# Held-back batch loads, v ahead of q and k, and a longer attention lead in a windowed-attention and feed-forward kernel

## The chip, the cores and the metric

The kernel runs on one core of a Trainium2 chip. TensorE (PE) does the matmuls, VectorE (DVE) and ScalarE (ACT) the elementwise work, and GpSimd (POOL) and SyncE (SP) issue nearly all DMA transfers of this kernel. The time of a run is the device time of that core in microseconds (us). Most comparisons below are between series of up to six runs of one kernel, taken on the same chip in turn with runs of the kernel before; each of the four series of experiments ran on another chip. A run is called slow when it is over 1.5% above the fastest of its kernel; all comparisons use the other runs, called fast. Each run also comes with its mean granted clock of TensorE, where 1.0 is full speed.

## The reference, cut to what matters

```python
# q, k, v: 8 batches x 8 heads x 576 positions x 64
scores = scale * np.matmul(q, k.transpose(0, 1, 3, 2))
scores = np.where(abs(i - j) <= 32, scores, -1e9)         # window of 32 to each side
out    = softmax(scores) @ v
x = out.transpose(0, 2, 1, 3).reshape(4608, 512)          # tokens x model width
h = x @ w_in                                              # 512 -> 2048
g = np.where(h > 0, h, np.exp(np.minimum(h, 0)) - 1)      # ELU
return g @ w_out                                          # 2048 -> 512
```

## The kernel before

A small planner written in Python lists every operation with an engine, a rank and its dependencies, simulates a rough timetable, and emits the instructions of each engine in that order. On the chip each engine keeps its order, and only data dependencies and buffers hold it back. The gates and estimated durations of the plan are not enforced.

The work is cut into 36 pairs of attention blocks (128 tokens each) and 10 token tiles for the feed-forward part (two tiles of 2 pairs, eight of 4). "Lead" is how far, in units of the plan of about a microsecond, a pair's attention is ranked ahead of its tile's feed-forward groups.

```python
PER = 8.0
LEAD = 20.0
def prank(i):                      # rank of the attention of pair i
    return PER * tiles[where[i][0]][0] + PER * (i - tiles[where[i][0]][0]) - LEAD - 16
LQ0, LQD = 52.0, 2.4               # loads of q and k: start and spacing in the plan
HR = sorted((..., ("H", t, fo)) for t ... for fo ...)      # feed-forward matmul groups by rank
def gate(r):                       # the last group ranked before r
    return [n for x, n in HR if x <= r][-1:]
# ... for batches 3 to 7: a gate in the plan alone, nothing on the chip
x = need - LQ0 + LQD * (2 * j + (nm == "q"))
deps += gate(x)
P.op(("LQ", b, nm, j), "POOL", 0.9, x, deps, lambda ...: load_nat(b, nm, j), ...)
# ...
def load_nat(b, nm, j):            # GpSimd issues the load of 128 rows of q or k
    ...
    nc.gpsimd.dma_start(out=live["N", nm, b][0:n, j, :]..., in_=src[128 * j:128 * j + n])
def XQ(b, nm, j):                  # SyncE turns them into qT, kT with a DMA transpose
    nc.sync.dma_start_transpose(dst, live["N", nm, b][0:n, j, :])
def load_v(b, qb):                 # GpSimd loads v; SyncE then makes shifted copies (vw<-vw)
    nc.gpsimd.dma_start(out=vt[r:r + hi - lo, qb, :, 0:D], in_=vb[lo:hi])
def X(i):                          # attention result of pair i, transposed to xt
    ...
    if i >= NPX:                   # NPX = 8
        nc.sync.dma_start_transpose(dst, xs)
        return
    pt = psT_p.tile(...)           # pairs 0 to 7: on TensorE, through the one psT bank
    ...
```

So SyncE's queue carries, in one order, the transposes of q and k (`kT<-bf`, `qT<-bf`), those of the attention result (`xt<-xs`), the shifted v copies and the outputs. The first feed-forward matmul of a tile needs the `xt` transpose of all its pairs. The buffers that TensorE writes are named ps: psS for scores, psO for attention times v, psT for transposes (one bank), psH for the first feed-forward matmul (three banks), psY for the second.

The softmax here doesn't subtract the row's maximum and nothing guards it: scores larger than these inputs give would overflow.

## Time and profile before

| | kernel before |
|---|---|
| median of the first runs | 338.19 us (336.65 to 339.34) |
| span of the profiled run, clock | 334.4 us, 1.000 |
| TensorE (PE) busy | 305.8 us |
| PE waits for `xt` | 7.1 us, four times |
| PE waits for `y` (output copies) | 2.3 us, six times |
| PE waits for the first q and k | 8.1 us |
| loads of k (128 KB), issue to landing | 8.4 us |

The prediction shows the main lines of this profile. One further view helps: the timeline of GpSimd (POOL) while it issues batch 5's loads. Columns: start us, length us, engine, line, operation, tile, and in brackets the idle time before it with what ended it.

```profile
98.72 0.88 POOL L304 DMA_DIRECT2D bf<-in_k_dram  x1 [8.84 <-DMA kT<-bf]
99.59 0.78 POOL L322 DMA_DIRECT2D vw<-in_v_dram  x1
100.40 0.97 POOL L304 DMA_DIRECT2D bf<-in_q_dram  x1
101.36 0.88 POOL L304 DMA_DIRECT2D bf<-in_k_dram  x1
...
```

GpSimd waits 8.84 us for a buffer (`kT<-bf` must have read it) and then issues load after load, one every 0.9 us. This is a burst.

### The profile page before, as it was taken

Reading aid. Unit: us, or ns where it says so; the run is one execution under the profiler, and the core shown is the slowest. Engines: PE = TensorE matmul, PEld = TensorE weight load, DVE = VectorE, ACT = ScalarE, POOL = GpSimd, SP = SyncE. Lnnn points to the kernel's source line nnn. Section 1 sums busy time; section 2 is a strip of 40 time slices with the busy share of each in tenths; the row PEclk is TensorE's granted clock in tenths of the full one; section 3 lists DMA queues with packets and bytes.
Section 4 is the critical chain, followed back from the end, with each engine's and each line's share of the span. In section 5 each row is a group of like instructions: output and inputs, shape, how many; then the busy total and the mean of one; then the engine's idle time right before and its main releaser. Section 6 shows DMA issues by size and latency. Waiting matters only on the chain.

```text
span 334.4 us, 7358 instructions
## 1 busy us (share of the span) xinstructions
PE 305.8 (91%) x2896; PEld 160.8 (48%) x2896; DVE 212.0 (63%) x500; ACT 195.5 (58%) x333; POOL 94.6 (28%) x130
## 2 busy tenths in 40 slices
PE   1589999799989998999799979999999999899995
PEld 1477666545544444444344434444444444344442
DVE  4586696568958776677576656667666766455400
ACT  2258997687755553655266636665666566465611
POOL 8944456964318500850095000000000000000000
PEclk9999999999999999999999999999999999999999
DMA  7999999999999998999999973633362111100021
GB/s 98 148 195 208 193 195 178 165 140 155 146 156 181 169 155 115 155 165 155 129 152 170 148 120 78 144 94 80 79 114 71 40 64 49 47 33 31 31 94 63
DMA packets 140369, 41.02 MB, mean 123 GB/s; under 512 B 125360, under 2 KB 135856, under 8 KB 140336
## 3 DMA queue, kind: packets, MB, share of 16 engines
q0 software_dynamic: 91872, 18.36, 72.9%
q1 hardware_dynamic: 48320, 22.08, 35.5%
q8 instruction: 22, 0.36, 0.5%
q10 hardware_dynamic: 144, 0.13, 0.1%
q14 instruction: 11, 0.09, 0.1%
HBM read 36.70 MB, written 9.44 MB: 138 GB/s over the span
## 4 chain that ended last, share of the span: by engine, by line
PE 71%; DMA 14%; DVE 6%; ACT 5%; issue 1%; SPq 1%; POOL 1%; ACTq 0%; POOLq 0%
PE psH L438 32%; PE psY L481 26%; DMA xt<-xs 10%; PE psO L391 4%; PE psS L358 3%; DMA bf<-in_k_dram 2%; DMA vw<-vw 2%; DVE xs L406 2%; PE psT L272 2%; ACT e L446 1%; PE psS L481 1%; PE psO L481 1%; PE psT L481 1%; ACT f L456 1%; ACT pu L366 1%
## 5 line engine op out<-in xcount | busy, mean ns | idle before, releaser
L438 PE MATMUL psH<-xt,w_in_sb 128*128 128x512 bf16 (+1 forms) x640 | 146.8, 360 | 7.4 <-DMA xt<-xs 7.1
L446 ACT ACTIVATE e<-psH 128x512 f32<-128x512 f32 (+1 forms) x160 | 88.3, 554 | 99.3 <-PE psH L438 94.9
L481 PE MATMUL psY<-w_out_sb,g 128*128 128x512 bf16 x528 | 132.9, 379 | 2.3 <-ACT y L491 2.3
L438 PEld LDWEIGHTS <-w_in_sb 128*128 128x128 bf16 x640 | 60.0, 99 | 65.9 <-issue 7.5
L481 PEld LDWEIGHTS <-g 128*128 128x128 bf16 x576 | 52.9, 98 | 58.8 <-issue 3.1
L464 DVE SCALAR_TENSOR_TENSOR g<-f,psH 128x512 bf16<-128x512 bf16 (+1 forms) x72 | 45.0, 625 | 32.9 <-ACT f L456 32.6
L458 DVE TENSOR_SCALAR f<-e 128x512 bf16<-128x512 f32 (+1 forms) x88 | 37.8, 429 | 39.2 <-ACT e L446 39.2
L467 DVE TENSOR_TENSOR g<-psH,f 128x512 bf16<-128x512 f32 (+1 forms) x88 | 56.5, 642 | 2.8
L456 ACT ACTIVATE f<-e 128x512 bf16<-128x512 f32 (+1 forms) x72 | 42.0, 583 | 2.1
L366 ACT ACTIVATE pu<-psS 128x1024 bf16<-128x1024 f32 x36 | 36.8, 1021 | 7.3 <-PE psS L358 5.9
L322 POOL DMA_DIRECT2D vw<-in_v_dram x40 | 33.8, 854 | 22.3 <-PE psH L438 4.0
L304 POOL DMA_DIRECT2D bf<-in_k_dram x25 | 21.6, 866 | 45.8 <-DMA kT<-bf 41.3
L391 PEld LDWEIGHTS <-pm 128*128 128x128 bf16 x576 | 27.0, 101 | 13.6 <-DMA vw<-vw 0.7
L406 DVE TENSOR_TENSOR xs<-psO,rc 128x256 bf16<-128x256 f32 x68 | 28.9, 424 | 2.4
L391 PE MATMUL psO<-vw,pm 128*128 128x65 bf16 x544 | 28.9, 196 | 0.7 <-DMA vw<-vw 0.4
L379 DVE TENSOR_TENSOR pm<-pu,masks 128x512 bf16<-128x512 bf16 x72 | 27.1, 418 | 3.2 <-ACT pu L366 3.2
L304 POOL DMA_DIRECT2D bf<-in_q_dram x25 | 21.8, 871 | 8.1 <-DMA bf<-in_q_dram 2.5
L404 DVE RECIPROCAL rc<-psO 128x4 f32<-128x4 f32 x68 | 12.3, 181 | 18.4 <-PE psO L391 17.8
L491 ACT COPY y<-psY 128x512 f32<-128x512 f32 x33 | 18.8, 570 | 4.5 <-PE psY L481 4.5
L358 PE MATMUL psS<-qT,kT 64*128 64x64 bf16 (+1 forms) x640 | 17.0, 199 | 3.1 <-ACT pu L366 1.8
L358 PEld LDWEIGHTS <-kT 64*128 64x128 bf16 (+1 forms) x640 | 12.1, 102 | 14.9 <-issue 11.9
L272 PEld LDWEIGHTS <-bf 64*64 64x64 bf16 x432 | 10.2, 123 | 14.4 <-DMA bf<-in_q_dram 5.8
(46 smaller groups left out, 87.6 us busy)
## 6 DMA issues: line engine op xcount, KB each, us to landing
out_dram<-y SPq DMA_DIRECT2D x35, 256.0 KB, 2.4
vw<-vw SPq DMA_DIRECT2D x12, 260.0 KB, 6.5
vw<-in_v_dram POOLq DMA_DIRECT2D x24, 128.0 KB, 11.7
bf<-in_k_dram POOLq DMA_DIRECT2D x20, 128.0 KB, 8.4
bf<-in_q_dram POOLq DMA_DIRECT2D x20, 128.0 KB, 8.8
w_in_sb<-in_moe_w_in_dram POOLq DMA_DIRECT2D x4, 512.0 KB, 10.0
w_out_sb<-in_moe_w_out_dram POOLq DMA_DIRECT2D x4, 512.0 KB, 13.9
bf<-in_q_dram POOLq DMA_DIRECT2D x6, 288.0 KB, 11.3
```

Of the source, the lines that this page charges most:

```text
L304: nc.gpsimd.dma_start(out=live["N", nm, b][0:n, j, :].rearrange("p (h d) -> p h d", d=D), in_=src[128 * j:128 * j + n])
L358: nc.tensor.matmul(psS[p0:p1, h % 2, s, hp, :], lhsT=kT[b % NKB][base:base + 64, hp, c:c + p1 - p0], rhs=rhs, start=True, stop=True)
L366: nc.scalar.activation(pu, live.pop(("S", i)), AX.Exp, scale=SCALE)
L391: nc.tensor.matmul(o[:, j, :], lhsT=p[:, h, s * QB:s * QB + 128], rhs=vw[b % NVB][:, qb, h, :], start=(s == 0), stop=(s == 1))
L406: nc.vector.tensor_mul(live["X", i][:, g * HP:(g + 1) * HP, :], o[:, :, 0:D], rb)
L438: nc.tensor.matmul(ps, lhsT=w_in_sb[:, do, fo * 128:(fo + 1) * 128], rhs=xts[t][:, do, :], start=(do == 0), stop=(do == NDO - 1))
L446: nc.scalar.activation(e, ps, AX.Exp)
L456: nc.scalar.activation(f, e, AX.Relu, bias=1.0, scale=-1.0)
L458: nc.vector.tensor_scalar(f, e, -1.0, 0.0, ALU.add, ALU.min)
L464: nc.vector.scalar_tensor_tensor(gs[t][:, fo, :], f, -1.0, ps, ALU.mult, ALU.max)
L467: nc.vector.tensor_tensor(gs[t][:, fo, :], ps, f, ALU.max)
L481: nc.tensor.matmul(ps, lhsT=gs[t][:, fo, c * 128:(c + 1) * 128], rhs=w_out_sb[:, fo, :], start=(fo == 0), stop=(fo == NFO - 1))
```

## The change

The intent was to make the loads of batches 3 to 7 spread out as the plan has them, so that the DMA transposes meet fewer loads, and to give these transposes more time before TensorE needs them.

```diff
+    scr = const.tile([1, 1], BF16)
...
-    def load_nat(b, nm, j):
+    def hold(g):
+        for _, t, fo in g:
+            nc.gpsimd.tensor_copy(scr, gs[t][0:1, fo, 0:1])
+
+    def load_nat(b, nm, j, g):
+        hold(g)
...
-    def load_v(b, qb):
+    def load_v(b, qb, g):
+        hold(g)
...
-    LEAD = 20.0
+    LEAD = (20.0, 28.0)
+    NLEAD = 8
...
-        return PER * tiles[where[i][0]][0] + PER * (i - tiles[where[i][0]][0]) - LEAD - 16
+        return PER * tiles[where[i][0]][0] + PER * (i - tiles[where[i][0]][0]) - LEAD[i >= NLEAD] - 16
...
-    LQ0, LQD = 52.0, 2.4
-    XQ0, XQD = 36.0, 3.5
+    LQ0, LQD = 64.0, 2.4
+    XQ0, XQD = 38.0, 3.0
...
-    HR = sorted((PER * tiles[t][0] + 2 * fo * tiles[t][1] / 4, ("H", t, fo))
+    HR = sorted((PER * tiles[t][0] + 2 * fo * tiles[t][1] / 4, ("GG", t, fo))
...
-                x = need - LQ0 + LQD * (2 * j + (nm == "q"))
+                n = 2 * j + (nm == "q")
+                x = need - LQ0 + LQD * (n + 5 if b > XB or n >= NV3 else n)
...
-            x = need - LQ0 + LQD * (10 + qb / 2)
+            x = need - LQ0 + LQD * (qb / 2 + (NV3 if b == XB else 0))
```

`hold` copies one element of a finished feed-forward group (`g`, written by VectorE), so GpSimd can't issue the load behind it before that group exists. The cut part has a new order of the first loads (a list called RING), and new estimates of DMA durations and of how transfers share the DMA engines in the planner.

## The prediction

> **What bounds the kernel now.** I read the totals of the page first. TensorE (PE) is busy for 305.8 of 334.4 us, at full granted clock, and no other engine passes 63%.
>
> ```profile
> span 334.4 us, 7358 instructions
> PE 305.8 (91%) x2896; PEld 160.8 (48%) x2896; DVE 212.0 (63%) x500; ACT 195.5 (58%) x333; POOL 94.6 (28%) x130
> ```
>
> So only the 28.6 us in which PE stands idle can be won, as long as its work stays the same. The second view, the waits of PE alone, says what those 28.6 us are. Its columns are the waiting instruction, what released it, total us, times, longest:
>
> ```profile
> PE psH L438 <- DMA xt<-xs: 7.1, 4, 2.3
> PE psT L272 <- DMA bf<-in_q_dram: 5.6, 2, 5.4
> PE psH L272 <- DMA bf<-in_k_dram: 2.5, 2, 2.2
> PE psY L481 <- ACT y L491: 2.3, 6, 1.0
> PE psT L272 <- ACT xt L427: 1.9, 3, 0.7
> PE psS L358 <- ACT pu L366: 1.8, 2, 1.1
> PE psT L421 <- ACT kT L290: 1.5, 2, 0.7
> ...
> PE psO L391 <- DMA vw<-vw: 0.4, 1, 0.4
> ```
>
> The two waits for q and k (8.1 us) belong to the first 12 us, when the first inputs are in flight. The largest wait after that is L438, the first feed-forward matmul of a tile of 512 tokens, waiting for `xt`: the attention result of the tile's last pair, transposed by a DMA on SyncE's queue. It happens four times, and the chain that ended last passes through the transpose each time. In order of time (start, length, what):
>
> ```profile
> 88.58 7.83 DMA xt<-xs
> 96.46 2.75 PE psH L438 x12
> ...
> 119.08 7.29 DMA xt<-xs
> 126.41 1.04 PE psH L438 x4
> ...
> 152.91 9.34 DMA xt<-xs
> 162.39 2.75 PE psH L438 x12
> ...
> 187.18 7.91 DMA xt<-xs
> 195.13 1.02 PE psH L438 x4
> ```
>
> The 40-slice view says why these transposes take 7 to 9 us. The loads are issued by GpSimd (POOL) in bursts, and end before the 200th us:
>
> ```profile
> POOL 8944456964318500850095000000000000000000
> DMA  7999999999999998999999973633362111100021
> ```
>
> The DMA engines are filled until then and mostly idle after. In the DMA view cut to 200-290 us the median transpose of `xt` lands in 2.4 us; in 60-100 us it takes 8.4. The tiles begun after 200 us never wait for it. So the bound is PE, with a secondary loss made by long DMA latency against a short lead.
>
> **What the Trainium skill says.** "DMA: Bandwidth & Descriptors", section "Issuing engines are not separate DMA queues", says that transfers started by SyncE, ScalarE or GpSimd run on the same 16 DMA engines and interleave. "Queues, rings and completion order" says that each engine takes turns between queues, a packet at a time. The trace agrees: 2.4 us alone against 8.4 us beside GpSimd's loads, though SyncE's transposes have a queue of their own. It also tells me that a shorter backlog in the load queue does not speed a transpose by itself; only moments without a load in flight do. "GPSIMD Engine Reference", section "Elementwise — side-by-side cycle accounting", says that GpSimd dispatches in two software steps where VectorE has one, so even one element has a fixed cost; the smallest GpSimd records here, memsets of one column, show 0.10 us. "SBUF — State Buffer", section "SBUF: two separate sides", says that GpSimd shares an SBUF port pair with VectorE, exclusively for a whole instruction. No line of this trace isolates such a collision.
>
> **The change, part by part.** I compared the instruction orders of both programs (orders, no times) and gave each PE piece its length in the trace: 0.86 us for four 128x512 matmuls, 0.34 for the scores of a pair, 0.24 for half its attention-times-v. PE's work is the same in both, so the sum on PE moves by 0.
>
> *Lead of 28.* Between the last attention product of a tile and the tile's first feed-forward matmul, PE has 6 or 7 groups of 0.86 us in the kernel before, and 13 or 14 after (8 for the tile of pairs 8 to 11, at whose first pair the lead begins). With the scores and attention pieces between them that is 6.1 to 7.2 us before, 12.4 to 13.3 after (7.2 and 8.3 for that first tile). What has to fit, read at the four waits from the end of the attention product to landing:
> - first tile: 87.50 to 96.41, 8.9 us
> - second: 118.38 to 126.37, 8.0 us
> - third: 152.20 to 162.25, 10.1 us
> - fourth: 186.48 to 195.09, 8.6 us
>
> With unchanged latencies the three later waits vanish (10.1 is under 12.4), and the first is left with about 8.9 - 8.3 = 0.6 us. Gain 7.1 - 0.6 = 6.5 us.
>
> *Holds.* 73 one-element reads on GpSimd. At an estimated 0.1 to 0.2 us each (from the 0.10 us memsets) that is 7 to 15 us on an engine that is 72% idle: 0 us on the path. Each lets a load go only when VectorE has finished a given feed-forward group. The kernel before asks for this order only in its plan; in its trace GpSimd runs ahead until a buffer stops it. Fifteen loads of a batch go out within 16 to 20 us there (98.7 to 117.5 for batch 5) and then GpSimd waits up to 17.1 us. After, one goes every 2.4 units of the plan, about 2.4 us (a tile is 32 units, and some 31 us of PE work), so a batch is spread over some 30 us. The bytes are the same, so the DMA engines will be less full between 70 and 200 us, and I expect transposes at 4 to 7 us rather than 7 to 9. That should remove half of the 0.6 left above: gain 0.3 us. By PE work from gate to use, the last q or k load of a batch is still about 45 us ahead of its scores, and the v loads 60 us ahead of use, against landings of 8 to 14 us: no new wait. The reverse cost is that VectorE may overwrite a feed-forward buffer only after GpSimd has read it; that is two tiles, some 65 us, later.
>
> *v ahead of q and k.* It removes the wait for the shifted v copies, 0.4 us.
>
> *More even order.* The six waits of L481 for `y` (2.3 us) mostly come where two output tiles stand nearly back to back. After the change an attention piece or feed-forward group usually stands between. I count 1.0 us; the 0.96 us wait at 289 us, in the tail, stays. The pairs of PE transposes that fight for the single `psT` bank (1.9 + 1.5 us) are somewhat better separated for batch 2; I count 0.7 us.
>
> *New order of the first loads.* Weights and first q, k and v are the same bytes through the same saturated queue. But PE now wants batch 1's first transposes before its first feed-forward group and batch 2's about 4 us earlier. By the landings read from the waits of GpSimd (first weights 18.7 us, third output-weight chunk 43.6 us, batch 2's q some 2 us sooner than before) these come within 1 us of need. I charge 0.8 us.
>
> Sum: -6.5 - 0.3 - 0.4 - 1.0 - 0.7 + 0.8 = -8.1 us. From the median of 338.2 that gives 330.1 us.
>
> **The rivals.** First: the wait only moves. With transposes hidden, PE would stall for VectorE or ScalarE, or on the load order between 30 and 65 us. For it: several arrivals there are just in time, and the two weight chunks, the second batch's q and the shifted v copies each could cost 1 us. Against it: in stretches of 10 us between 90 and 290 us VectorE is at 54 to 87% and ScalarE at 45 to 68%, and PE is busy without a gap in most of it. It would give 332 to 335 us.
>
> Second: the holds make loads too late, or spread them so that every transpose meets a load. A landing would have to pass 12 us from attention product to use; the worst now is 10.1. For it: SyncE issues in order, so a q or k transpose that waits for a late load also holds back the `xt` transpose behind it. Against it: 14 us and more lie between a load's gate and its transpose's planned place. It would keep half of the waits: 334 to 338 us.
>
> Third: the start also gains, because the v loads no longer stand behind the mask building and the DMA rate dips from 10 to 15 us are filled. Against it: the first transposes are released by q and k, which do not move. It would give 327 to 328.5 us.
>
> **Range and chances.** The central sum is 8.1 us, most of it in one well-read term (6.5). The small terms and the early order may err by 2 us either way, and the runs of before spread by 2.7 us. So 326.8 to 334.5. Two per cent is 6.8 us, or 331.4; the estimate is 1.3 us beyond, so faster by over 2% gets 0.66, within 2% 0.31, slower 0.03.
>
> **What would show it right or wrong.** Right: the `xt` row vanishes from PE's waits or shrinks below 1 us, PE's busy time stays at 306 us, span near 326 us; GpSimd's busy digits are spread to the 200th us and its idle time ends with VectorE's groups rather than with `kT` transposes. Wrong: a PE wait for `bf`, `w_out_sb`, `kT` or `vw` after 24 us of more than 2 us, or psH waiting for VectorE; more PE idle between 24 and 70 us than the 3.5 us of before; or `xt` landings over 11 us.

## The result, and the profile after

In the first series the changed kernel took 326.73 us in the median of four runs (330.86, 328.39, 324.47 and 325.06), the kernel before 337.66. The ratio of the fast runs is 0.9649, with a 95% interval of 0.9556 to 0.9743. Ratios here are those over fast runs of the same rounds; they are not quite the ratio of the medians or means quoted. The kernel is faster by 3.5%, and a little faster than the lower end of the predicted range. A second series of the same kernel (label after_again) had a median of 324.54, a ratio of 0.9592 (0.9549 to 0.9636) and only one run above 325.

The profile of that second series is read here, because it ran at a clock of 1.000 like the profile of before. (It fell on the slowest of its six runs, 327.1 us; the spans of the others were some 2 to 3 us shorter.) First the totals of the page, the busy digits of GpSimd and of the DMA engines in 40 slices, and the new row of the held reads:

```profile
span 325.0 us, 7515 instructions
PE 304.1 (94%) x2896; PEld 160.1 (49%) x2896; DVE 210.4 (65%) x500; ACT 196.3 (60%) x333; POOL 108.0 (33%) x203
...
POOL 8944446945455454153356445000000000000000
...
DMA  7999999999999999999999999832112221000021
...
L308 POOL COPY scr<-g 1x1 bf16<-1x1 bf16 x73 | 14.9, 204 | 54.4 <-DVE g L481 44.9
```

GpSimd's digits no longer alternate between bursts and zeros. The 73 reads take 0.20 us each. The DMA engines are not emptier, although the prediction had expected it: their digits stay at 9 to the 200th us as before. Only the order in time of the loads changed, not their sum.

Then PE's waits:

```profile
PE psT L435 <- ACT kT L297: 2.5, 3, 1.3
...
PE psH L452 <- DMA xt<-xs: 1.2, 1, 1.2
...
```

The `xt` row has gone from 7.1 us to 1.2, and what is left is one wait, at the tile of pairs 8 to 11, the first whose `xt` comes by DMA transposes. It is called the first tile from here on, as in the prediction. The row of `y` (2.3 us before) is gone. The wait for `psT` at L435 has risen from 1.5 to 2.5 us, while that of the other user of this bank (L272 before, L279 after) fell from 1.9 to 0.4.

Last, the timeline of GpSimd answering to the burst shown of before:

```profile
118.71 0.88 POOL L317 DMA_DIRECT2D bf<-in_q_dram  x1 [0.57 <-issue]
119.65 0.24 POOL L308 COPY scr<-g 1x1 bf16<-1x1 bf16 x1
120.10 0.87 POOL L317 DMA_DIRECT2D bf<-in_k_dram  x1 [0.21 <-issue]
123.48 0.24 POOL L308 COPY scr<-g 1x1 bf16<-1x1 bf16 x1 [2.51 <-DVE g L481]
123.94 0.87 POOL L317 DMA_DIRECT2D bf<-in_q_dram  x1 [0.21 <-issue]
```

Each load has its read in front, and the read is ended by VectorE's group: 2.51 us of idle time in one case, none in another. One load goes out about every 2.2 us (eight between 116.1 and 131.8 us) where it was every 0.9.

The slowest run of the first series (330.86 us) is worth a look, since it was profiled (span 329.0 us, clock 0.993); for the other slower one, 328.39 us at clock 1.000, there is no trace. On the chain of the profiled one that ended last, in order of time (start, length, what):

```profile
89.73 8.86 DMA xt<-xs
...
98.63 1.48 PE psH L452 x4
100.11 0.44 PE psO L405 x8
100.55 2.75 PE psH L452 x8
```

The `xt` transpose stood in SyncE's queue for 2.1 us (its data was ready at 87.61 us) and then took 8.86 us. PE waited 3.2 us, and its next 12 feed-forward matmuls took 1.48 + 2.75 = 4.23 us where 12 normally take 2.59 (three times 0.86). In windows of 0.05 us PE's granted clock falls to 0.50 at 99.1 us, some 0.4 us after the wait has ended, and is back at 1.00 at 102.5.

### The profile page after: what moved, and what is told of

It is laid out like the page before. It is cut to its first block, busy times and chain, and to the rows that moved or that the text cites. A ratio compares the mean times of both kernels' runs of the same rounds, so it can differ in the third digit from the quotient of the medians.

```text
span 329.0 us, 7515 instructions
## 1 busy us (share of the span) xinstructions
PE 306.6 (93%) x2896; PEld 161.1 (49%) x2896; DVE 210.8 (64%) x500; ACT 196.6 (60%) x333; POOL 108.1 (33%) x203
## 4 chain that ended last, share of the span: by engine, by line
PE 84%; DMA 6%; POOL 4%; ACT 2%; DVE 2%; issue 1%; ACTq 0%; POOLq 0%
PE psH L452 37%; PE psY L495 34%; PE psO L405 5%; DMA bf<-in_q_dram 3%; PE psS L372 3%; DMA xt<-xs 3%; PE psT L279 2%; PE psS L495 1%; PE psO L495 1%; PE psT L495 1%; POOL vw L336 1%; POOL bf L267 1%; ACT e L460 1%; PE psT L435 1%; ACT kT L297 1%
## 5 line engine op out<-in xcount | busy, mean ns | idle before, releaser
L452 PE MATMUL psH<-xt,w_in_sb 128*128 128x512 bf16 (+1 forms) x640 | 150.9, 365 | 3.4 <-DMA xt<-xs 3.2
L308 POOL COPY scr<-g 1x1 bf16<-1x1 bf16 x73 | 14.8, 203 | 58.0 <-DVE g L481 48.3
L317 POOL DMA_DIRECT2D bf<-in_q_dram x25 | 21.0, 840 | 5.3 <-issue 4.1
L418 DVE RECIPROCAL rc<-psO 128x4 f32<-128x4 f32 x68 | 12.3, 181 | 14.6 <-PE psO L405 14.1
L372 PEld LDWEIGHTS <-kT 64*128 64x128 bf16 (+1 forms) x640 | 12.1, 102 | 14.9 <-issue 11.9
## 6 DMA issues: line engine op xcount, KB each, us to landing
w_in_sb<-in_moe_w_in_dram POOLq DMA_DIRECT2D x4, 512.0 KB, 12.4
w_out_sb<-in_moe_w_out_dram POOLq DMA_DIRECT2D x4, 512.0 KB, 13.8
```

The source lines that it names most:

```text
L317: nc.gpsimd.dma_start(out=live["N", nm, b][0:n, j, :].rearrange("p (h d) -> p h d", d=D), in_=src[128 * j:128 * j + n])
L372: nc.tensor.matmul(psS[p0:p1, h % 2, s, hp, :], lhsT=kT[b % NKB][base:base + 64, hp, c:c + p1 - p0], rhs=rhs, start=True, stop=True)
L452: nc.tensor.matmul(ps, lhsT=w_in_sb[:, do, fo * 128:(fo + 1) * 128], rhs=xts[t][:, do, :], start=(do == 0), stop=(do == NDO - 1))
```

## The experiments

Fifteen runs were made in four series. In the texts on record, where theories have letters, D is that the loads have to be spread over the whole batch (a late start of a burst isn't enough), and E is that PE's clock falls after a long wait and so makes a lost microsecond cost more. "Mean" is that of the fast runs. The clock column is the range over the runs of that kernel.

| label | what it is | median us | mean us | ratio (95%) | clock |
|---|---|---|---|---|---|
| after_again | the changed kernel | 324.54 | 324.84 | 0.9592 (0.9549 to 0.9636) | 1.000 |
| no_hold | changed, no reads | 330.93 | 330.50 | 0.9760 (0.9713 to 0.9807) | 0.988 to 1.000 |
| no_lead | changed, lead 20 | 328.73 | 328.63 | 0.9705 (0.9667 to 0.9743) | 1.000 |
| lead_only | before, lead 28 | 334.47 | 334.78 | 0.9888 (0.9838 to 0.9937) | 0.990 to 0.995 |
| hold_only | before, with reads | 327.54 | 327.50 | 0.9683 (0.9638 to 0.9729) | 0.998 to 1.000 |
| v_behind | changed, v behind q, k | 324.66 | 324.75 | 0.9602 (0.9556 to 0.9648) | 0.997 to 1.000 |
| no_hold_npx12 | no_hold, 4 more pairs on PE | 326.71 | 326.94 | 0.9667 (0.9619 to 0.9714) | 0.998 to 1.000 |
| t3lead36 | changed, lead 36 for pairs 8 to 11 | 325.24 | 325.38 | 0.9610 (0.9559 to 0.9662) | 0.996 to 1.000 |
| hold_first | before, one read a batch | 331.91 | 331.97 | 0.9832 (0.9792 to 0.9872) | 0.999 to 1.000 |
| hold_lead | before, reads and lead | 323.90 | 324.19 | 0.9602 (0.9562 to 0.9641) | 0.998 to 1.000 |
| old_ring | changed, old first loads | 329.46 | 327.14 | 0.9682 (0.9577 to 0.9787) | 0.993 to 1.000 |
| before_again | the kernel before | 338.46 | 338.21 | 1.0017 (0.9947 to 1.0087) | 0.993 to 0.999 |
| v_first_burst | changed, one read a batch | 330.98 | 331.29 | 0.9774 (0.9724 to 0.9825) | 0.988 to 0.995 |
| hold_lead_psh | hold_lead, transposes of pairs 4 to 7 in psH | 323.28 | 323.29 | 0.9538 (0.9493 to 0.9583) | 0.998 to 1.000 |
| hold_lead_psh2 | hold_lead, half of batch 2's in psH | 323.48 | 323.75 | 0.9557 (0.9505 to 0.9608) | 1.000 |

The kernel before had fast means of 338.64, 338.32, 337.64 and 338.95 us in the four series. All kernels gave correct results.

### First series: the parts taken out, and the lead alone

after_again is the changed kernel without an edit.

> The changed kernel once more, for more runs and a profile in its fast state. The profile on record fell in a slow run (329.0 us) with one wait of 3.2 us for xt, at the first tile with the new lead, followed by some 3.4 us of matmuls at 0.37 us instead of 0.22. Theory A (that wait and its slow matmuls are what separates slow from fast runs): a fast profile has a wait below 1.5 us there, no slow matmuls, and a span of 322 to 324 us. Rival: the wait stays at 3 us in fast runs too, and the runs differ in the first 70 us. Time against the kernel before: 0.960 to 0.970 either way.

It was read above. The next one keeps the plan and drops the reads:

```diff
     def hold(g):
-        for _, t, fo in g:
-            nc.gpsimd.tensor_copy(scr, gs[t][0:1, fo, 0:1])
+        return
```

> The changed kernel with the 73 one-element reads left out; the order on every engine is the same (the plan is the same). Theory A (the lead alone covers the transposes, the holds are worth under 0.5 us, as predicted): within 1 us of the changed kernel, transposes of xt at 7 to 9 us between 100 and 200 us, and still no waits for xt after the first tile, because 12.4 us lie between. Theory B (the holds carry the gain by shortening the transposes): 4 us or more slower than the changed kernel, with PE waits for xt, or SyncE held by q and k transposes behind long loads.

Measured: a mean of 330.50 us, 5.7 us over after_again. The median `xt` transpose lands in 9.8 us between 60 and 100 us and in 7.7 between 100 and 200 (after_again: 7.6 and 5.2). Yet there is just one wait for `xt`, of 4.4 us, at the first tile; at the later tiles the lead hides even such transposes. In SyncE's queue before that wait, and then on the chain that ended last:

```profile
84.14 2.62 SPq L326 DMA_TRANSPOSE qT<-bf  x1
86.85 2.66 SPq L326 DMA_TRANSPOSE kT<-bf  x1
89.60 1.29 SPq L430 DMA_TRANSPOSE xt<-xs  x1
```

```profile
89.60 8.44 DMA xt<-xs
...
98.08 1.30 PE psH L451 x4
99.39 0.44 PE psO L404 x8
99.83 2.93 PE psH L451 x8
```

The data of that `xt` transpose was ready at 85.86 us, but it was issued only at 89.60: for 3.7 us it stood behind two q and k transposes whose issue took 2.6 us each. In the kernel before, the same transpose was issued 0.2 us after its data. From the end of the attention product (85.19) to landing (98.04) it is 12.9 us, against 8.5 us in which PE had work; that is the wait of 4.4. After the wait, 12 matmuls took 1.30 + 2.93 = 4.23 us in place of 2.59. The wait thus cost 4.4 + 1.6 = 6.0 us. Theory B has the time right, and its mechanism too, but at one tile alone.

```diff
-    LEAD = (20.0, 28.0)
+    LEAD = (20.0, 20.0)
```

> The changed kernel with the lead at 20 for all pairs. By the order, 7.2 to 8.3 us of PE work lie between the last attention product and the first feed-forward matmul of a tile, instead of 12.4 to 13.3. Theory A (the lead carries the gain): the four waits for xt return, 5 to 7 us slower than the changed kernel. Theory B (the holds carry it): transposes land in 4 to 5 us, with 1 us before their issue that fits into 7.2, so at most 1.5 us slower than the changed kernel.

Measured: 328.63 us, 3.8 over after_again, between the two theories. There is no wait for `xt` at all, with transposes of 5.8 and 4.8 us in the two stretches. What comes back is the wait for output copies, to the tenth the same as in the kernel before:

```profile
PE psY L495 <- ACT y L505: 2.3, 6, 1.0
```

lead_only is the kernel before with only these lines changed:

```diff
-    LEAD = 20.0
+    LEAD = (20.0, 28.0)
+    NLEAD = 8
...
- ... - LEAD - 16
+ ... - LEAD[i >= NLEAD] - 16
```

> The kernel before with the lead of 28 from pair 8 on and nothing else. Its plan still takes the old load times, and by its order only 6.8 to 9.5 us of PE work lie between the last attention product and the first feed-forward matmul of the tiles that waited (6.1 to 7.2 before). With transposes at 7 to 9 us and 1 us ahead of them, theory A expects 2 to 4 us of the 7.1 us of waits gone: 334 to 336 us. Theory B: nothing gained, 337 to 338 us, as the loads come in the same bursts. If the constant alone gave all, it would be 330 us or less.

Measured: 334.78 us, only 3.9 less than before. That lies in the range of theory A, but not for its reason: the waits for `xt` did not shrink, and it is the row of `y` that fell, from 2.3 to 0.4 us. The waits for `xt` still sum to 7.1 us, now in two: 4.8 us at the first tile and 2.3 at the one that begins at 194 us. At the first, the transpose stood in SyncE's queue for 4.2 us (ready at 86.47, issued at 90.68). First the chain, then the windows of this stretch (start:end, length, busy us of each engine with instruction counts, PE's granted clock, DMA share, GB/s):

```profile
90.68 8.85 DMA xt<-xs
...
99.57 5.17 PE psH L438 x12
```

```profile
96.00:98.00 2.00, 0.00 (x0) 0.00 (x0) 0.17 (x1) 0.00 (x0) 0.00 (x0) 0.92 1.83 101
98.00:99.00 1.00, 0.00 (x0) 0.00 (x0) 0.00 (x0) 0.00 (x0) 0.41 (x1) 0.50 1.72 153
```

The clock falls to 0.50 within the wait (at 97.7 us, and for 6.8 us), and 12 matmuls take 5.17 us, double the usual 2.59. The Trainium skill describes this in "TensorE: Matmul & The Clock Gate", section "What's actually happening": TensorE goes to half rate after an idle window of some 3.4 us and needs about as long a busy stretch to come back. The trace agrees in kind. A second thing is seen in the order of the instructions: with the old estimates in the planner, lead 28 gives gaps of only 6.8 to 9.5 us of PE work at five of the seven tiles that have DMA transposes, not the 12.4 of the changed kernel. The number in the source isn't the lead that the program gets.

### Second series: the reads alone, v behind, and the first tile

hold_only is the kernel before with the `hold` of the diff and with gates on the finished groups ("GG"), nothing else.

> The kernel before with the one-element reads in front of its loads of batches 3 to 7 (gated on the feed-forward group that the old plan already names), old lead, old order of v, old plan constants. By its order 6.1 to 7.2 us of PE work lie between the last attention product and the next tile. Theory B (spread loads shorten the transposes to about 5 us; 0.7 us lie ahead of them): the four waits for xt shrink to 0 to 0.5 us each, no drop of the granted clock, 329 to 331 us. Theory A (only the lead covers them): at least half of the waits stay, 334 us or more.

Measured: 327.50 us, 10.8 less than before in the same series, with all other parts of the change left out. The loads and transposes of the 60 to 100 us stretch, in the DMA view (KB of each, median us to landing):

```profile
bf<-in_k_dram POOLq DMA_DIRECT2D x4, 128.0 KB, 5.4
...
xt<-xs SPq DMA_TRANSPOSE x5, 4.4
```

In the kernel before these were 10.6 and 8.4 us. The gap between the last attention product and the first feed-forward matmul is 6.1 to 7.7 us in the trace of hold_only, at the tiles that have DMA transposes. The `xt` transpose of the first tile is issued at once when its data is ready (87.77 and 87.80 us). At 4.4 us a transpose fits into it without any added lead, and PE's row of `xt` waits is gone, as is that of `vw`. The row of `y` stays at 2.3.

The kept traces also say what the reads change for a transpose. From the issue and landing times one can count how many of GpSimd's loads are in flight, in the mean, beside an `xt` transpose:

| profile, stretch | loads in flight | `xt` to landing, median |
|---|---|---|
| no_hold, 60 to 100 us | 7.8 | 9.8 us |
| before, 60 to 100 us | 6.3 | 8.4 us |
| after_again, 60 to 100 us | 4.6 | 7.6 us |
| before, 100 to 200 us | 3.8 | 7.0 us |
| lead_only, 100 to 200 us | 2.1 | 4.5 us |
| hold_only, 60 to 100 us | 1.8 | 4.4 us |
| before, 200 to 290 us | 0.0 | 2.4 us |

So a transpose is shorter where fewer loads are in flight beside it, and in lead_only also without reads. The busy digits of the DMA engines don't show this: before 200 us they are 9 in nearly every slice of all these profiles. There is scatter (in the slow profile of the changed kernel 4.1 loads go with 8.9 us), and SyncE's own other transfers in flight fall along with the loads (4.1 to 2.2 from before to hold_only, 60 to 100 us), so the two are not told apart.

```diff
-                x = need - LQ0 + LQD * (n + 5 if b > XB or n >= NV3 else n)
+                x = need - LQ0 + LQD * n
...
-            x = need - LQ0 + LQD * (qb / 2 + (NV3 if b == XB else 0))
+            x = need - LQ0 + LQD * (10 + qb / 2)
```

> The changed kernel with the loads of v behind those of q and k again, holds and lead kept. The order of PE around the tiles is the same. If v ahead is worth only the wait for shifted v (0.4 us), as predicted: within 1 us of the changed kernel, 324 to 326 us. Rival: with v late, the shifted copies and the SyncE queue (five q and k transposes now stand ahead of the last xt of the first tile, where three did) cost more: 327 us or more, with the wait at the first tile at 4 us or more.

Measured: 324.75 us against 324.84. The order of v against q and k has no effect that shows here.

no_hold_npx12 is no_hold with `NPX = 12`: pairs 8 to 11, those of the first tile, are transposed on PE instead.

> The changed kernel without holds, and with the attention result of pairs 8 to 11 transposed on PE instead of by DMA, as pairs 0 to 7 are. This adds 4 transposes of some 0.25 us each on PE and 4 copies of 0.58 us on ScalarE. Theory C (all that the holds are worth beside the lead is the one wait at the first tile of 512 tokens, 4.4 us, and the slow clock after it): 325 to 327 us against 330.5 without holds alone, clock 1.0. Rival (longer transposes also cost at later tiles): 329 us or more.

Measured: 326.94 us, so 3.6 less than no_hold (means of different series), although PE does more work and the remaining `xt` transposes still take 7 us or more. Its clock is back at 0.998 to 1.000. So, with the lead in place and the reads left out, most of the loss is that one wait: 3.6 of the 5.7 us come back, and the four transposes that PE now does are another 1 us or so by the estimate above.

t3lead36 gives pairs 8 to 11 alone a lead of 36:

```diff
- ... - LEAD[i >= NLEAD] - 16
+ ... - (LEAD[i >= NLEAD] + 8.0 * (8 <= i < 12)) - 16
```

> The changed kernel with a lead of 36 for pairs 8 to 11, 28 after. By the order 10 groups of 0.86 us, some 11 us of PE work, lie ahead of the first tile that waits (8 groups in the changed kernel), and its last xt transpose stands ahead of two of the q and k transposes. If the wait left at that tile (1.2 and 3.2 us in two profiles) is the main thing left: no wait for xt in the profile, 322 to 324 us. Rival: pairs 8 to 11 come before their data, and waits for kT, qT or vw of the same size take its place: 324 to 327 us.

Measured: 325.38 us, the same as the changed kernel within its spread. No wait for `xt` is left, and no gain either: once the reads are there, little is to be had at that tile.

### Third series: is it the late start or the spreading?

hold_first is hold_only with the read kept only before the first k load of a batch (`if nm == "k" and j == 0: hold(g)`) and none before v. Each batch starts as late as with all reads, but as a burst.

> The kernel before with holds in front of only the first load of each of batches 3 to 7: the same order on every engine as with all loads held (327.5 us there), the same start of each batch, but its other fourteen loads go out as fast as buffers allow. Theory D (it is the spreading that shortens the transposes, since fewer loads are in flight beside each): transposes of xt and q/k at 7 to 9 us, loads at 8 to 14 us again, waits for xt back, granted clock below 1 in some runs, 334 to 339 us. Rival (it is the later start of a batch that moves its loads away from the tile's end): 327 to 329 us.

Measured: 331.97 us, between what the two theories expected. No wait for `xt` came back; its transposes landed in 2.5 us between 60 and 100 us, as four of the five were issued before the burst. But the burst that begins at 89.85 us met the shifted v copies on SyncE's queue:

```profile
96.81 8.63 DMA vw<-vw
...
135.28 8.50 DMA vw<-vw
```

PE waited 3.0 us for them. So theory D, as it was put, fell for `xt`: where a burst lies in time decides which transfer it delays. A burst still cost 4.5 us against the spread loads of hold_only (means of two series, on two chips, where the kernel before agrees within 0.7 us).

hold_lead is hold_only plus the lead lines of lead_only: no new order of first loads, no v ahead, no new planner estimates.

> The kernel before with holds and with the lead of 28 from pair 8 on, but with its old plan constants, old order of the first loads and v last. If holds (10.8 us alone) and lead (the 2.3 us of waits for y, and perhaps 0.7 us) are the whole change: 324 to 325.5 us, no waits for y after 70 us. If the new plan constants or the new order of the first loads add something of their own: 326.5 us or more.

Measured: 324.19 us, a ratio of 0.9602 against 0.9592 for the whole change. Within the intervals the reads and the lead are the whole of it; that the other parts cancel among themselves is not excluded.

old_ring is the changed kernel with the order of the first loads of the kernel before.

> The changed kernel with the old order of the first loads (batches 0 to 2 and weights). I charged the new order 0.8 us in the prediction. In the profiles the stretch from 24 to 70 us has 4.4 to 5.0 us of PE waits with the new order, 3.2 to 3.6 with the old. So 323.5 to 325 us, 0 to 1 us faster than the changed kernel. Rival: the new order is a gain at the start, and this run is 1 us or more slower.

Measured: two kinds of runs. Its fastest, 324.61 us at clock 1.000, equals the changed kernel; four of six lay at 329.2 to 330.8 with clocks of 0.993 to 0.995. The profile fell on one at 0.998 and shows one wait of 2.6 us at the first tile without slow matmuls after it. As hold_lead keeps the old order too and had no such run, the order of the first loads can't be called good or bad from this. Inconclusive.

before_again was to catch the kernel before in a run of low clock.

> The kernel before itself, for another profile. Its timed runs lie between 335.4 and 343.2 us, and the granted clock falls from 1.0 to 0.98 as they get longer; the profile that I read had clock 1.0 and was one of the fastest. Theory E (in most runs one wait for xt passes 3 us or so, after which matmuls run at a lower granted clock for a while): this profile has a clock below 0.996, one or more waits of over 3 us, and matmuls of over 0.3 us behind it. Rival: the waits are as in the first profile, and the clock falls elsewhere.

Measured: the profile fell on a run of 338.11 us with clock 0.999, which shows the same four `xt` waits (6.8 us, the longest 2.5) and no slow matmuls. So half-rate stretches in the kernel before are not seen in a profile. What the record of its runs says is this: in the 44 runs of the kernel before made beside the experiments, those with a clock of 0.998 or more (8 runs) took 336.5 us in the mean; 0.990 to 0.997 (17 runs) 339.2; 0.985 to 0.989 (13 runs) 340.4; and below (6 runs) 343.2. A straight line through them has 348 us per unit of clock lost. If a stretch at half rate costs as much time as it takes from the clock's mean, one expects about the span itself, some 336 us. Also, the 44 clocks lie in five groups with gaps between (0.979 to 0.980, 0.983 to 0.985, 0.988 to 0.990, 0.993 to 0.995, 0.998 to 1.000). By an estimate from the traces, a low stretch of 3.4 us takes 1.7 / 336 = 0.005 from the mean, which is the step between groups (the profiled runs with one such stretch show 0.993 and 0.991, those with two 0.990 and 0.989). This fits theory E, but it is a correlation: the test that theory E was put to, this profile, did not show it.

### Fourth series: the burst with v in front, and a better version

v_first_burst is the changed kernel with one read a batch, before its first v load, and none before q and k. The v copies can't be hit by the burst, as v goes first.

> The changed kernel (v ahead, long lead) with a hold in front of only the first v load of each of batches 3 to 7; the other fourteen loads of a batch follow as fast as buffers allow. Theory F (a batch that starts late enough needs no spreading, if v is ahead and the lead is long): 324.5 to 326 us, no waits for vw or xt. Theory D (spreading is needed): a wait for xt of 3 us or more at the first tile as without holds, 329 to 331 us.

Measured: 331.29 us, 6.5 over the changed kernel (means of different series, on two chips). The burst now hits the first tile's transpose:

```profile
97.18 1.89 PE psH L452 x4
...
99.51 3.41 PE psH L452 x8
```

A wait of 2.8 us came before these lines. 12 matmuls then took 5.3 us instead of 2.59. In windows of 0.05 us the clock is at 0.50 from 96.4 to 103.2 us: it fell 2.0 us after PE had gone idle, within the wait. So with either order of v a burst costs 4.5 to 6.5 us, and the spreading itself is needed: D holds in this weaker form.

The two last runs aim at the psT bank, whose waits (2.6 us in hold_lead) are what is left between 24 and 70 us. hold_lead_psh gives the PE transposes of pairs 4 to 7 a bank of the three of psH:

```diff
-        pt = psT_p.tile([128, NDO, 128], BF16, name="psT", tag="psT")
+        pool, tag = (psH_p, "psH") if i >= 4 else (psT_p, "psT")
+        pt = pool.tile([128, NDO, 128], BF16, name=tag, tag=tag)
```

> The kernel before with holds and lead (323.9 us, equal to the changed kernel), with the PE transposes of the attention results of pairs 4 to 7 put into a psH bank instead of the single psT bank that they share with the transposes of batch 2. If the psT bank makes the waits of 2.6 us between 24 and 70 us: these fall below 1 us and the time to 321.5 to 323 us, faster than both kernels by 0.3 to 0.8%. Rival: the feed-forward matmuls then wait for a psH bank instead, 324 us or more.

hold_lead_psh2 moves half of batch 2's q and k transposes instead:

```diff
-        pool, tag = (psH_p, "psH") if b == 0 and n % 4 else (psT_p, "psT")
+        pool, tag = (psH_p, "psH") if b == 0 and n % 4 or b == 2 and n % 2 else (psT_p, "psT")
```

> As the run before, but with every second transposed tile of batch 2 in psH instead of those attention results. Same theory, 321.5 to 323.5 us; rival: the feed-forward groups between are held by the psH banks, 324 us or more.

Measured: 323.29 and 323.75 us, with ratios of 0.9538 and 0.9557, both just above the range expected. PE's idle time between 24 and 70 us (46 us less its busy time) was 2.1 and 2.0 us, against 2.7 in hold_lead, 3.4 before and 4.4 in after_again. In hold_lead_psh a wait of psH for VectorE took part of what psT lost:

```profile
PE psH L429 <- DVE g L475: 1.4, 2, 1.2
```

hold_lead_psh is the fastest kernel: 4.6% under the kernel before, and some 0.5% under the changed one. The last figure compares two series whose intervals overlap, so it is likely rather than settled.

## Why the prediction was right or wrong

**What held.** The bound is PE's own work, and the `xt` waits were the largest loss that could be removed: 7.1 us before, 1.2 in the profile of after_again, none in that of v_behind. The gaps were read about rightly (6.1 to 7.2 us before by the order, 6.1 to 7.9 in the trace). The three later waits vanish through the lead even with the long transposes of no_hold. The 73 reads cost 14.9 us of GpSimd's time, the upper end of the estimated 7 to 15, and none on the path. Nor did they disturb VectorE: its `xs` instructions take 424 ns before and after. Neither the loads nor VectorE became late by much: after the first 12 us PE waits for `bf` only once, 1.4 us at 24.7 us, never for `vw`, and for VectorE at psH 0.4 us (a sign of being wrong by the prediction's own list, but a small one). The estimate of 4 to 7 us for transposes beside spread loads is met between 100 and 200 us (5.2 in after_again) and missed between 60 and 100 (7.6, with 4.6 loads in flight); hold_only has 4.4 there. By the constants in the source the changed plan starts its loads earlier than no_lead (by 8 units; 5.8 us there) and hold_lead (by 12; 4.6 us). That fits, but it was not varied alone.

**The step that failed.** In the prediction it reads: "With unchanged latencies the three later waits vanish (10.1 is under 12.4), and the first is left with about 8.9 - 8.3 = 0.6 us", and from it "gain 0.3 us" for the holds. no_hold is that very case, and its first wait was 4.4 us, with 1.6 us of slow matmuls behind it: 6.0 us, ten times the estimate. The gap was read rightly (8.5 us of PE work against 8.3). The latency was not unchanged: 12.9 us in place of 8.9. Of the 4.0 us more, the transpose itself gave 0.6 (8.44 against 7.83), and the time in SyncE's queue 3.5 (3.7 against 0.2). An earlier attention product makes the transpose ready earlier, but here it became ready while q and k transposes were being issued, and SyncE takes them in order. The prediction had taken from before a latency that held the queue of before. And it took the cost of a wait as its length, while in four traces (waits of 2.8, 3.2, 4.4 and 4.8 us) the clock halved in the wait or just after it. With the reads, this queueing is 1.7 us in after_again and none in hold_only.

So the term that was mis-sized is that of the holds, 0.3 us, which measures 5.7 beside the lead. Without that term the prediction comes to 330.4 us, and no_hold, the kernel without the holds, took 330.50. That the other terms together fit so well is partly luck: the lead leaves 6.0 us at the first tile where they have 0.6, and they have too little for the `y` waits and nothing for the low clock of the kernel before.

**The sums of the two main parts.** Measured by the means:

| part | taken alone, from before | beside the other part |
|---|---|---|
| holds | 338.32 - 327.50 = 10.8 us | 330.50 - 324.84 = 5.7 us |
| lead | 338.64 - 334.78 = 3.9 us | 328.63 - 324.84 = 3.8 us |

The prediction gave the lead the credit first and asked what was left for the holds. By its own numbers a transpose of 4 to 7 us against a gap of 6.1 to 7.2 us would have been nearly hidden by the holds alone, and hold_only shows it. What the lead gives beside the holds is mostly another thing, the `y` waits: they are 2.3 us in before, no_lead and hold_only, and 0.4 or none in lead_only, hold_lead and after_again. The prediction had put 1.0 us of them down to "more even order"; the term was right in kind and too small by 1.3 us.

**The base.** The savings were read in a profile with clock 1.000 and taken from the median of all runs. Yet most runs of the kernel before are at lower clocks: its fast runs average 338.4 us, the eight runs at 0.998 or more 336.5. The difference of 1.9 us also went with the change, since all kernels with reads before every load but old_ring keep 0.996 or more in the runs made beside the experiments. Of the terms left out it is one of the largest; with the `y` waits (1.3 us more than counted) and PE's busy time (1.7) it brought the result below the range, by 0.1 us in the median of the first series and by 2.3 in after_again. That the low clock of before comes from half-rate stretches after long waits is argued from the correlation and from four other traces, not shown in a trace of before.

**The small terms.** v ahead was to give 0.4 us and gives nothing that v_behind can show, because the `vw` wait goes with the reads alone. The 0.7 us at psT came out as 0.5: the two rows fell from 1.9 + 1.5 to 0.4 + 2.5 us. Yet PE's idle time between 24 and 70 us rose from 3.4 to 4.4 us, which the prediction named as a sign of error. So the charge of 0.8 us for the early order was right in kind: after_again waits 1.4 us at 24.7 us for batch 1's q, 0.4 for VectorE and 0.3 for an output weight, none of which the kernel before does there. Whether the new order costs or gains in sum stays open: hold_lead, without it, equals the whole change, and old_ring was inconclusive.

**The account.** Between the means of the first series lie 338.64 - 324.84 = 13.8 us. Between the profiled runs lie 336.33 - 327.10 = 9.2: `xt` waits are 5.9 of them (7.1 to 1.2), `y` waits 2.3, and PE's busy time 1.7 (305.8 to 304.1), less some 0.7 us that other waits add. Of the remaining 4.6 us, 2.3 lie in that the profiled run of before was below its mean (most of it the base, above), and 2.3 in that the profiled run of after_again was above its own; no trace shows why. PE's busy time, with the same 2896 instructions, goes with the reads: 305.5 to 306.0 in before, before_again and hold_first, 303.5 to 304.9 in the profiles with a read before every load and no low stretch of the clock. Why was not isolated and stays open.

**The rivals.** The first (the wait only moves) was right about the load order at the start, by 1 us of idle time. The second (loads too late, transposes held in SyncE's order) named the mechanism behind the first tile's wait, but it is strongest where the reads are missing, not where they are. The third (a gain at the start) gave the right total for the wrong reason: PE's wait for the first q and k was 8.1 us before and 7.3 in after_again, but its busy time in the first 24 us was the same (12.2 and 12.3 us).

## What to carry to other kernels

When two parts of a change attack the same wait, work out each alone as well as one after the other. A wait can cost more than its length when TensorE's clock falls with it, as in the four traces here; the extra cost did not grow with the length (1.6 us on 12 matmuls after 4.4 us, 2.7 after 2.8), so count the slow matmuls in the trace. And a gate that exists only in a plan holds nothing back on the chip; a one-element read of the right buffer did, at 0.20 us on an engine that was idle for two thirds of the span.

## What the Trainium skill lacked or had wrong

- "TensorE: Matmul & The Clock Gate", sections "What's actually happening" and "Why this matters for your kernels": they put the drop to half rate after an idle window of about 3.4 us, the window running freely, and advise against gaps over about 3 us. The low stretches here fit windows of that length: 3.4 us (the profile of the slow run, no_hold) and 6.8 us (lead_only, v_first_burst). But the clock fell once after only 2.0 us without a matmul (v_first_burst, a wait of 2.8 us), so a whole idle window was not needed, nor a gap over 3 us. A wait of 2.6 us (old_ring) and the waits of up to 2.5 us of the kernel before left it at 1.00, as did the 5.4 us at the start of that profile. With the fall at 2.0 us after PE went idle in one trace and at 3.6 us in another (the slow run), these runs give no single length as the limit.
- "DMA: Bandwidth & Descriptors", section "DMA Transpose (X-bar)": it gives no time for a single transpose of 128x512 next to loads. Here it took 2.4 us with no load in flight, 4.4 us with some two, 7.6 with 4.6, and 8.4 to 9.8 with six to eight, with the DMA digits at 9 in nearly every slice of all but the first case.
- The same page, section "Issuing engines are not separate DMA queues": it calls the sequencer's time to start a DMA usually small relative to the DMA itself. On SyncE a transpose took 1.2 to 1.4 us to issue in the median, with and without reads, and single ones up to 3.8 (lead_only), against 2.4 us for the lone transfer. In no_hold a transpose waited 3.7 us behind two whose issue took 2.6 us each.
- "GPSIMD Engine Reference", section "Elementwise — side-by-side cycle accounting": it has no figure for the smallest copy. Here a one-element copy took 0.20 us, 73 times.
